# Turning the keys of two batches with one DMA transpose per group of heads

## Chip, cores and metric

One core of one Trainium2 chip runs the program. The metric is the device time of one execution in microseconds (us), the median of three runs. A profiled execution of the same program gives the span (first to last instruction) and the trace from which all rows are taken.

## The reference

Talking-heads attention followed by a gated MLP with spatial mixing, batch B = 4, H = 12 heads, S = 448 positions, D = 64 per head, all inputs and outputs fp32:

```python
scores = scale * np.matmul(q, k.transpose(0, 1, 3, 2))
scores = np.einsum('bhij,hg->bgij', scores, w_pre)
attn = softmax(scores)
attn = np.einsum('bhij,hg->bgij', attn, w_post)
x = np.matmul(attn, v)                       # then (b, s, h*d)
h = gelu(x @ w_in); u, v = split(h)
v_s = w_sg @ layer_norm(v) * g_ln + b_sg
out = x + (u * v_s) @ w_out
```

Matrix products are made of fp16 high and low halves (three products for one fp32 product), or of fp32 operands in the two head mixes where the kernel chooses so.

## The kernel before, in words

**Tiling.** Queries are worked on in chunks: four per batch, of 64, 128, 128 and 128 rows (the first batch a little otherwise, `RUNS`). For each chunk and pair of heads TensorE multiplies qT by kT (`qk_mm`, line 919), ACT and DVE split the scores into halves in the tile s, and SP writes them to a scratch tensor in DRAM (s_d, line 958). They are read back with the heads of ten queries in the partitions (tile g, `load_pair`, line 1019, loads at 1031 and 1037), mixed over heads on TensorE (ps_s), reduced and exponentiated (DVE line 1077, ACT line 1084), mixed again (`postmix`, TensorE tile at), and multiplied by v (ps_av). The MLP of a batch (ps_v, ps_u, ps_x) runs on TensorE between the attention of the next one.

**Keys and queries.** kT holds, for each of three groups of four heads (`hg`, HG = 4), the transposed keys: high and low half (index t), two pairs of heads (index a), 448 columns. For batches 0 and 1 the transposes are made on TensorE (`turns`, line 586). For batches 2 and 3 (`b >= B_DT`) they are made by DMA: `load_k` (line 560) loads four heads of k into a staging buffer st32 (two buffers, ring "st", loads at lines 548 and 550), an engine casts them to the high halves and subtracts for the low halves into the staging buffer st16 (one buffer, ring "sp"; POOL lines 442 and 445 in this program), and `turns_by_dma` (line 567) issues eight DMA transposes on SP: for each half and each pair of heads one of three full blocks of 128 rows (line 580) and one of the last 64 rows (line 582). The load of the next group is planned only when both rings are free, so after the transposes of the group before. The chunks' queries of these batches go through the same single buffer st16 and one DMA transpose of 12 blocks each (`load_q`, line 489). So each batch has three groups of keys, six in all, and four chunks of queries.

**Order.** Nothing is scheduled at run time: a planner (`class Plan`, line 260) simulates the engines with hand-written costs and lists each engine's instructions; each engine then works its list off in order, waiting on semaphores. A step has an engine, a cost, a rank (its due time) and a condition. To each rank a random jitter is added (`JIT` = 0.2, from `random.Random(SEED)`). For a step on SP the cost is the time on the DMA engines, or a pair (that time, number of issues); SP is charged 370 ns for each issue (`SP_ISSUE`), and the planned landing follows from both. SP issues nearly all the kernel's DMAs: writes and reads of scores, loads of k, q, v and weights, transposes, outputs.

**Softmax form.** In the later three batches the second head mix runs with fp16 halves of the probabilities in two of three pairs of query groups and with fp32 operands in the third (`P_F32`).

Of the kernel before, what the change touches and what calls it, by code (L numbers as in the profile page):

```python
# [11 lines left out]
F16 = mybir.dt.float16  # L12
# [31 lines left out]
N_P32 = 3  # L44
N_PRE = 8
C_PRE = 800
SEED = 129
JIT = 0.2
SPIN = 110
SPIN_GAP = 200  # L50
# [57 lines left out]
def talking_heads_gmlp(ctx, tc, q, k, v, w_pre, w_post, w_in, g_ln, w_sg, b_sg, w_out, out):  # L108
    nc = tc.nc
    B, H, S, D = q.shape  # L110
# [3 lines left out]
    P = 128  # L114
# [3 lines left out]
    NC = S // TC  # L118
    JF = S // P
    JL = S - JF * P  # L120
    NA = JF * H + H // 2
    CQ = 120
    NCH = (S + CQ - 1) // CQ
# [13 lines left out]
    HG = 4  # L137
# [6 lines left out]
    ORD = (0, 1, 2, 3)  # L144
# [13 lines left out]
    const = ctx.enter_context(tc.tile_pool(name="const", bufs=1))  # L158
# [55 lines left out]
    mskc_t = vn_hi.rearrange("p c f -> p (c f)")[:, 504:520].bitcast(F32)  # L214


    kT = const.tile([P, H // HG, 2, HG // 2, S], F16, name="kT")
    qT2 = [const.tile([P, 2, H // 2, P], F16, name=f"qT{i}") for i in range(2)]
    v32 = const.tile([P, NA, D], F32, name="v32")
    at32 = const.tile([P, NA, AW], F32, name="at32")  # L220
# [39 lines left out]
    class Plan:  # L260
# [8 lines left out]
        def __init__(self):  # L269
# [7 lines left out]
            self.size = {}  # L277
            self.rnd = random.Random(SEED)

# [6 lines left out]
        def free(self, *names):  # L286
            return self.after([self.res.get(n, 0) for n in names])

        def seen(self, *names):
            return self.after([self.tm.get(n) for n in names])  # L290
# [4 lines left out]
        @staticmethod  # L295
        def after(times):
            return None if None in times else max(times)
# [6 lines left out]
        def give(self, t, *names):  # L304
            for n in names:
                assert self.res[n] is None, n
                self.res[n] = t
# [95 lines left out]
    def ones(n):  # L403

        return {"act": 100 + 0.9 * n, "dve": Shared(70 + 0.52 * n), "pool": 75 + 1.06 * n}
# [28 lines left out]
    free, seen, past, after, take, give, chain = pl.free, pl.seen, pl.past, pl.after, pl.take, pl.give, pl.chain  # L434


    def cast(o, i, scale=1.0, e=None):
        e = e or pl.on
        if e is nc.scalar:
            e.activation(out=o, in_=i, func=AF.Copy, scale=scale)  # L440
        else:
            e.tensor_scalar(out=o, in0=i, scalar1=scale, scalar2=1.0, op0=ALU.mult, op1=ALU.mult)  # L442

    def diff(o, a, b, e=None):
        (e or pl.on).tensor_tensor(out=o, in0=a, in1=b, op=ALU.subtract)  # L445
# [8 lines left out]
    def turn(ps, src, width):  # L454

        for n, x in enumerate(src):
            rows = x.shape[0]
            tr(ps[:, n * width:n * width + rows], x, ident32[:rows, :rows])
# [6 lines left out]

    def turn_k(hg, t, a, ps):
        turn(ps, [t[:, a, cc] for cc in range(JF)] + [t[:JL, a, JF]], P)
        return (ps[:, :S], *(kT[:, hg, k, a, :] for k in range(2)))

    def load_q(i):  # L470
        rank = K_Q12[i - 1] if i < 3 else fin[i - 1] - K_Q
# [49 lines left out]
    def load_kv():  # L521
        todo = [(b * GPB + (0, 3, 6)[hg] + (3 if b else 0), "v", b, hg) for b in range(B) for hg in range(H // HG)]
        for b in range(1, B):
            i = NCH * b - 1
            for hg in range(H // HG):
                todo.append((fin[i] + hg * HG * (fin[i + 1] - fin[i]) // H - K_KV, "k", b, hg))
        todo.sort()
        for rank, kind, b, hg in todo:
            if kind == "v":
                if ("v", b, hg) not in tm:  # L530
                    t = yield "sp", 2000, rank, 0, lambda: seen(("av", b - 1, ORD[-1])) if b else 0
                    fetch_v(b, hg, t)
                continue
            t = yield "sp", 2000, rank, 0, lambda: free(ring("st"), ring("sp"))
            load_k(b, hg, rank + 1, t)

    def fetch_v(b, hg, t):
        hs = slice(hg * HG, (hg + 1) * HG)
        nc.sync.dma_start(out=v32[:, hg * HG * JF:(hg + 1) * HG * JF].rearrange("p (h c) d -> p h c d", c=JF),
                          in_=v[b, hs, :JF * P].rearrange("h (p c) d -> p h c d", c=JF))  # L540
        if hg == H // HG - 1:
            for f in range(2):
                nc.sync.dma_start(out=v32[f * JL:(f + 1) * JL, JF * H:], in_=v[b, f * H // 2:(f + 1) * H // 2, JF * P:].rearrange("h p d -> p h d"))
        tm["v", b, hg] = t

    def fetch_k(b, h0, x):
        hs = slice(h0, h0 + HG)
        nc.sync.dma_start(out=x[:, :, :JF], in_=k[b, hs, :JF * P].rearrange("h (p c) d -> p h c d", c=JF))
        for f in range(2 if b else 1):
            nc.sync.dma_start(out=x[f * JL:(f + 1) * JL, :, JF], in_=k[b, hs, JF * P:].rearrange("h p d -> p h d"))  # L550
# [9 lines left out]
    def load_k(b, hg, rank, t0):  # L560
        h0 = hg * HG
        x, xname = staged("st")
        y, name = staged("sp")
        k32 = y.rearrange("p t a c b d -> p (t a c b d)").bitcast(F32).rearrange("p (a c e) -> p a c e", a=2, c=NC)
        fetch_k(b, h0, x)

        def turns_by_dma(t):
            for part in range(2):
                t = yield None, (ones, twos)[part](HG * NC * D), rank, t
                for a in range(2):  # L570
                    o = y[:, part, :, :, a, :]
                    if part:
                        diff(o, x[:, a::2], y[:, 0, :, :, a, :])
                    else:
                        cast(o, x[:, a::2])
            give(t, xname)
            t = yield "sp", (2500, 5), rank, t, lambda: seen(("qk", NCH * b - 1, h0 + HG - 1))
            for w in range(2):
                for a in range(HG // 2):
                    nc.sync.dma_start_transpose(out=kT[:, hg, w, a, :JF * P].rearrange("p (c j) -> p c j", c=JF),  # L580
                                                in_=y[:, w, a, :JF].rearrange("p c b d -> p (c b d)"))
                    nc.sync.dma_start_transpose(out=kT[:, hg, w, a, JF * P:], in_=y[:JL, w, a, JF].rearrange("p b d -> p (b d)"))  # L582
            give(t, name)
            tm["k", b, hg] = t

        def turns(t):
            t = yield None, ones(HG * NC * D), rank, t
            for a in range(2):
                side(pl.on, k32, x, a)
            give(t, xname)  # L590
            ends = []
            for a in range(2):
                t1 = yield "pe", 4 * C_TR, rank, t, lambda: after([work_free(), seen(("qk", NCH * b - 1, h0 + HG - 1))])
                ps, bank_name = work_bank("ps_k")
                split(rank, t1, turn_k(hg, k32, a, ps), S, bank_name, ends)
            give(t1, name)
            yield None, {"pool": 0}, rank, t1, lambda: max(ends) if len(ends) == 2 else None
            tm["k", b, hg] = max(ends)

        pl.add((turns_by_dma if b >= B_DT else turns)(t0))  # L600
# [6 lines left out]
    def ring(kind):  # L607
        return f"{kind}{stn[kind] % {'st': 2, 'sp': 1}[kind]}"

    def staged(kind):  # L610

        name = ring(kind)
        stn[kind] += 1
        take(name)
        if kind == "st":
            return st32.tile([P, HG, NC, D], F32, tag="st", name="st32"), name
        return st16.tile([P, 2, HG // 2, NC, 2, D], F16, tag="sp", name="st16"), name
# [196 lines left out]
    def work_free():  # L814
        return free(f"wk{works[0] % 2}")
# [47 lines left out]
    def part_mm(s, hg, ps):  # L863
        for n, (tq, tk) in enumerate(((0, 0), (0, 1), (1, 0))):
            for o in range(2):
                for a in range(2):
                    r = slice(a * D, (a + 1) * D)
                    m = QP * (2 * o + a)
                    mm(ps[m:m + QP, :S], lhsT=qT2[0][r, tq, 2 * hg + o, PART[s]:PART[s] + QP],
                                     rhs=kT[r, hg, tk, o, :], start=(n == 0), stop=(n == 2))  # L870

    def part_hi(s, hg, ps, eng=None):
        cast(e0[s][:, hg, 0], ps[:, :S], 1.0 / math.sqrt(D), eng)
# [45 lines left out]
    def qk_mm(i, h, pss):  # L919

        rows = q_rows(i)
        for n, (tq, tk) in enumerate(((0, 0), (0, 1), (1, 0))):
            for o in range(heads(i) // 2):
                w = 64 if quarters(i) else rows
                for c in range(0, rows, w):
                    m = min(w, rows - c)
                    for a, ps in enumerate(pss):
                        r = slice(a * D, (a + 1) * D)
                        mm(ps[o * rows + c:o * rows + c + m, :S], lhsT=qT2[i % 2][r, tq, h // 2 + o, c:c + m],
                                         rhs=kT[r, h // HG, tk, h // 2 % 2 + o, :], start=(n == 0), stop=(n == 2))  # L930

    def qk_place(i, h):
        if (i, h) in early:
# [106 lines left out]
    st = {}  # L1040
# [556 lines left out]
    with tc.manual_schedule():  # L1597
# [13 lines left out]
        for i, w in enumerate((w_pre, w_post)):  # L1611
# [4 lines left out]
                              in_=ident32[:H, :H].unsqueeze(1).unsqueeze(1).to_broadcast([H, 2, NH, H]))  # L1616
# [201 lines left out]
```

## Time and profile before

| | us |
|---|---|
| median of 3 runs | 606.68 |
| lowest, highest of them | 606.08, 610.87 |
| the profiled execution | 607.23 |
| its span | 605.5 |
| TensorE busy in it | 564.6 |
| VectorE (DVE), ScalarE (ACT), GpSimd (POOL) busy | 394.1, 397.1, 284.3 |
| mean granted TensorE clock, share of full | 0.975 |

Times in rows are counted from the start of the span. PE is TensorE, PEld its weight loads, SPq the queue of SyncE, which issues DMAs; a DMA's row on SPq is the time that its issue took. "idle before <-releaser" is how long the engine stood before the instruction and what ended that; of several things waited for, the last by the profile is named, which can be another than the one that mattered.

### The profile page before, as it was taken

To read this page: it belongs to the slowest core of one execution; us is meant where nothing else is said; L and a number is where in the kernel's file an instruction comes from. 1 tells how busy PE (TensorE), PEld (TensorE's weight loads), DVE (VectorE), ACT (ScalarE), POOL (GpSimd) and SP (SyncE) were. 2 spreads that over 40 slices of the span, in tenths; PEclk is the share of its full clock that TensorE was granted. 3 is DMA by queue.
4 is the path that set the end of the run, shared out by engine and by line. 5 is a ranking of instruction groups with operands and counts; after the bars stand their busy time and mean duration, and the time that the engine had idled before them with its cause. 6 is when DMAs were issued, how large, how long until landed. Compare 5 with 4: busy or idle time off the path is not lost.

```text
span 605.5 us, 24600 instructions
## 1 busy us (share of the span) xinstructions
PE 564.6 (93%) x10333; PEld 361.0 (60%) x10333; DVE 394.1 (65%) x991; ACT 397.1 (66%) x952; POOL 284.3 (47%) x421
## 2 busy tenths in 40 slices
PE   8999999999999989299999968789999999999997
PEld 4555666667656546146756635447666656678654
DVE  5866577766887765168878646447678786455560
ACT  5768787886776765256877638446768786765331
POOL 6425255764567572324735735545535474344100
PEclk9999999999999999599999997979999999999999
DMA  8989889995899556689897564689787555430002
GB/s 188 243 249 275 275 259 240 261 273 163 258 265 260 119 158 175 161 215 250 203 282 202 147 208 119 172 195 272 148 241 217 148 180 164 121 87 2 2 2 92
DMA packets 110607, 113.41 MB, mean 187 GB/s; under 512 B 60852, under 2 KB 97724, under 8 KB 110496
## 3 DMA queue, kind: packets, MB, share of 16 engines
q1 hardware_dynamic: 110432, 111.84, 68.3%
q8 instruction: 81, 1.33, 1.0%
q14 instruction: 30, 0.25, 0.1%
q10 hardware_dynamic: 64, 0.00, 0.0%
HBM read 64.20 MB, written 42.10 MB: 176 GB/s over the span
## 4 chain that ended last, share of the span: by engine, by line
PE 47%; SPq 3%; DMA 2%; ACT 1%; DVE 1%; issue 1%; POOL 1%; ACTq 0%; POOLq 0%
PE ps_x L236 9%; PE at L236 8%; PE ps_v L236 7%; PE ps_u L236 7%; PE ps_av L236 6%; PE ps_s L236 5%; PE ps_qk L236 4%; SPq L580 1%; SPq L582 1%; DMA g<-s_d 1%; ACT p L1084 0%; DMA s_d<-s 0%; DMA kT<-st 0%; DVE s L949 0%; ACT at L440 0%
## 5 line engine op out<-in xcount | busy, mean ns | idle before, releaser
L1084 ACT ACTIVATE p<-ps_s,nm 128x448 f32<-128x448 f32 x180 | 113.9, 634 | 33.3 <-DVE nm L1077 30.6
L1077 DVE TENSOR_REDUCE nm<-ps_s 128x1 f32<-128x448 f32 x180 | 105.7, 617 | 41.6 <-PE ps_s L236 41.4
L440 ACT ACTIVATE at<-at 128x420 f32<-128x420 f32 x178 | 97.8, 565 | 32.8 <-PE at L236 31.7
L440 ACT ACTIVATE s<-ps_qk 128x448 f16<-128x448 f32 (+3 forms) x145 | 72.1, 547 | 26.5 <-PE ps_qk L236 21.3
L236 PE MATMUL ps_qk<-kT,qT 64*64 64x448 f16 (+2 forms) x756 | 70.1, 360 | 19.0 <-DMA qT<-st 11.1
L236 PE MATMUL ps_av<-at,v 128*64 128x120 f32 (+3 forms) x1536 | 71.5, 262 | 0.1
L236 PEld LDWEIGHTS ps_av<-at,v 128*64 128x64 f32 (+1 forms) x1536 | 64.8, 136 | 9.3 <-issue 5.8
L236 PEld LDWEIGHTS at<-wp,p 64*64 64x64 f32 (+1 forms) x2580 | 57.1, 139 | 19.3 <-issue 7.4
L442 POOL TENSOR_SCALAR p<-p,rs 128x448 f16<-128x448 f32 (+1 forms) x56 | 39.3, 705 | 54.7 <-DVE rs L1090 33.3
L236 PE MATMUL at<-wp,p 64*64 64x60 f32 (+2 forms) x2580 | 61.7, 224 | 2.8 <-ACT at L440 2.6
L949 DVE SCALAR_TENSOR_TENSOR s<-ps_qk,s 128x448 f16<-128x448 f32 x84 | 48.8, 618 | 22.5 <-ACT s L440 21.2
L236 PE MATMUL ps_u<-xTh,wbuf 128*128 128x256 f16 (+1 forms) x384 | 60.7, 260 | 0.0
L1089 DVE TENSOR_SCALAR rs<-ss 128x1 f32<-128x1 f32 x180 | 26.9, 149 | 49.0 <-ACT p L1084 46.2
L236 PEld LDWEIGHTS <-wbuf 128*128 128x128 f16 x576 | 50.3, 98 | 12.3 <-issue 8.0
L236 PE MATMUL ps_x<-wo,gbuf 128*128 128x384 f16 (+1 forms) x336 | 57.4, 331 | 0.2 <-POOL gbuf L445 0.2
L442 POOL TENSOR_SCALAR wp<-wpc,rs 128x60 f32<-128x60 f32 x63 | 23.2, 368 | 68.8 <-DVE rs L1090 67.5
L236 PEld LDWEIGHTS <-qT 64*64 64x64 f16 (+2 forms) x756 | 23.2, 99 | 54.0 <-issue 24.4
L1113 DVE SCALAR_TENSOR_TENSOR p<-p,rs,p 128x448 f16<-128x448 f32 x58 | 44.7, 773 | 9.3 <-POOL p L442 5.8
L236 PE MATMUL ps_u<-xTl,wbuf 128*128 128x192 f16 (+1 forms) x192 | 49.8, 259 | 0.0
L236 PEld LDWEIGHTS <-p 64*128 64x128 f16 (+1 forms) x2610 | 38.3, 101 | 16.4 <-issue 8.4
L236 PE MATMUL ps_s<-g,wpre 60*64 60x448 f32 x324 | 43.7, 558 | 1.8 <-ACT p L1084 1.8
L236 PEld LDWEIGHTS <-gbuf 128*128 128x128 f16 (+1 forms) x384 | 30.6, 102 | 23.3 <-issue 7.7
(224 smaller groups left out, 1094.5 us busy)
## 6 DMA issues: line engine op xcount, KB each, us to landing
g<-s_d SPq DMA_DIRECT2D x166, 210.0 KB
s_d<-s SPq DMA_DIRECT2D x18, 448.0 KB
s_d<-s SPq DMA_DIRECT2D x24, 280.0 KB
v<-in_v_dram SPq DMA_DIRECT2D x12, 384.0 KB
out_dram<-ot SPq DMA_DIRECT2D x24, 192.0 KB
s_d<-s SPq DMA_DIRECT2D x18, 252.0 KB
s_d<-s SPq DMA_DIRECT2D x18, 224.0 KB
s_d<-s SPq DMA_DIRECT2D x18, 196.0 KB
```

Of the source, the lines that this page charges most:

```text
L236: nc.tensor.matmul(ps, lhsT=lhsT, rhs=rhs, **kw)
L440: e.activation(out=o, in_=i, func=AF.Copy, scale=scale)
L442: e.tensor_scalar(out=o, in0=i, scalar1=scale, scalar2=1.0, op0=ALU.mult, op1=ALU.mult)
L580: nc.sync.dma_start_transpose(out=kT[:, hg, w, a, :JF * P].rearrange("p (c j) -> p c j", c=JF), in_=y[:, w, a, :JF].rearrange("p c b d -> ...
L582: nc.sync.dma_start_transpose(out=kT[:, hg, w, a, JF * P:], in_=y[:JL, w, a, JF].rearrange("p b d -> p (b d)"))
L949: nc.vector.scalar_tensor_tensor(out=e[:, 1, :], in0=ps[:n, :S], scalar=1.0 / math.sqrt(D), in1=e[:, 0, :], op0=ALU.mult, op1=ALU.subtract)
L1077: nc.vector.tensor_reduce(out=nm, in_=st[n]["s2"][:, :S], axis=AX.X, op=ALU.max, negate=True)
L1084: nc.scalar.activation(out=x["p32"], in_=x["s2"][:, :S], func=AF.Exp, bias=x["nm"], accum_out=x["ss"])
L1089: nc.vector.tensor_scalar(out=x["rs"], in0=x["ss"], scalar1=1e-9, scalar2=1.0 / S_P, op0=ALU.add, op1=ALU.mult)
L1113: nc.vector.scalar_tensor_tensor(out=x["pl"], in0=x["p32"], scalar=x["rs"], in1=x["ph"], op0=ALU.mult, op1=ALU.subtract)
```

## The change

kT's columns are padded from 448 to 512, so that a group's 2 halves x 2 pairs x 4 blocks of 128 x 128 lie in one row of equal blocks; the eight transposes of a group become one of 16 blocks, whose last block of each pair is now turned with all its 128 rows (the rows beyond 448 are filled by the load and not read). Readers of kT take the first 448 columns. The planner is told another cost for the key loads (three issues), the last v load of a batch (three issues) and the transposes, and its random seed is another.

```diff
-SEED = 129
+SEED = 23
...
-    kT = const.tile([P, H // HG, 2, HG // 2, S], F16, name="kT")
+    kT = const.tile([P, H // HG, 2, HG // 2, NC * P], F16, name="kT")
...
-        return (ps[:, :S], *(kT[:, hg, k, a, :] for k in range(2)))
+        return (ps[:, :S], *(kT[:, hg, k, a, :S] for k in range(2)))
...
-                    t = yield "sp", 2000, rank, 0, lambda: seen(("av", b - 1, ORD[-1])) if b else 0
+                    t = yield "sp", (2400, 3) if hg == H // HG - 1 else 2000, rank, 0, lambda: seen(("av", b - 1, ORD[-1])) if b else 0
...
-            t = yield "sp", 2000, rank, 0, lambda: free(ring("st"), ring("sp"))
+            t = yield "sp", (2200, 3), rank, 0, lambda: free(ring("st"), ring("sp"))
...
-            t = yield "sp", (2500, 5), rank, t, lambda: seen(("qk", NCH * b - 1, h0 + HG - 1))
-            for w in range(2):
-                for a in range(HG // 2):
-                    nc.sync.dma_start_transpose(out=kT[:, hg, w, a, :JF * P].rearrange("p (c j) -> p c j", c=JF),
-                                                in_=y[:, w, a, :JF].rearrange("p c b d -> p (c b d)"))
-                    nc.sync.dma_start_transpose(out=kT[:, hg, w, a, JF * P:], in_=y[:JL, w, a, JF].rearrange("p b d -> p (b d)"))
+            t = yield "sp", (2800, 5), rank, t, lambda: seen(("qk", NCH * b - 1, h0 + HG - 1))
+            nc.sync.dma_start_transpose(out=kT[:, hg].rearrange("p t a (c j) -> p (t a c) j", c=NC),
+                                        in_=y.rearrange("p t a c b d -> p (t a c b d)"))
...
-                                     rhs=kT[r, hg, tk, o, :], start=(n == 0), stop=(n == 2))
+                                     rhs=kT[r, hg, tk, o, :S], start=(n == 0), stop=(n == 2))
...
-                                         rhs=kT[r, h // HG, tk, h // 2 % 2 + o, :], start=(n == 0), stop=(n == 2))
+                                         rhs=kT[r, h // HG, tk, h // 2 % 2 + o, :S], start=(n == 0), stop=(n == 2))
```

## Rows read from the trace of the kernel before

**Rows 1.** The page: busy time of the engines.
```profile
PE 564.6 (93%) x10333; PEld 361.0 (60%) x10333; DVE 394.1 (65%) x991; ACT 397.1 (66%) x952; POOL 284.3 (47%) x421
```

**Rows 2.** Windows: length, busy PE PEld DVE ACT POOL, then clock, DMA share, GB/s.
```profile
50.00:200.00 150.00, 144.91 (x2561) 95.26 (x2562) 108.77 (x289) 116.38 (x288) 84.51 (x129) 1.00 0.89 250
200.00:300.00 100.00, 85.71 (x1777) 52.50 (x1776) 61.33 (x153) 60.43 (x148) 45.97 (x59) 0.93 0.74 186
...
350.00:400.00 50.00, 35.68 (x662) 21.41 (x655) 24.00 (x59) 23.52 (x55) 22.51 (x28) 0.84 0.61 169
400.00:550.00 150.00, 149.44 (x3132) 97.66 (x3125) 104.11 (x274) 108.58 (x265) 75.11 (x106) 1.00 0.63 173
```

**Rows 3.** TensorE's waits, whole span: waited for: us in total, times, longest.
```profile
PE ps_qk L236 <- DMA qT<-st: 11.1, 1, 11.1
PE ps_s L236 <- ACT p L1084: 9.0, 2, 7.2
PE ps_qk L236 <- DMA kT<-st: 6.2, 3, 2.2
```

**Rows 4.** Chain of waits from 335 to 400 us, by line.
```profile
by line: SPq L580 10.1%; SPq L582 9.4%; DMA g<-s_d 8.8%; PE ps_x L236 8.2%; PE at L236 7.2%; issue 6.6%; PE ps_qk L236 5.5%; PE ps_av L236 5.1%; PE ps_s L236 4.7%; DMA s_d<-s 3.9%; DMA kT<-st 3.6%; SPq L1037 3.0%; SPq L550 2.7%; ACT p L1084
```

**Rows 5.** Timeline of SP's queue: start, duration, line, operation.
```profile
213.82 1.63 SPq L580 DMA_TRANSPOSE kT<-st  x1
...
223.88 1.23 SPq L582 DMA_TRANSPOSE kT<-st  x1
...
227.55 0.42 SPq L548 DMA_DIRECT2D st<-in_k_dram  x1
...
250.27 1.25 SPq L489 DMA_TRANSPOSE qT<-st  x1
...
340.02 1.19 SPq L580 DMA_TRANSPOSE kT<-st  x1
...
353.99 0.42 SPq L548 DMA_DIRECT2D st<-in_k_dram  x1
...
384.59 2.11 SPq L580 DMA_TRANSPOSE kT<-st  x1
```

**Rows 6.** Windows, columns as in rows 2: inside the fourth group's transposes.
```profile
344.00:352.00 8.00, 8.00 (x175) 4.58 (x173) 6.79 (x18) 6.87 (x19) 7.23 (x9) 1.00 0.20 39
```

**Rows 7.** Tile kT: its DMA transposes, ns min/median/max, first and last start.
```profile
L580 SPq DMA_TRANSPOSE kT<-st x24: 1193/1248/2497, 192.6 to 393.2; - x24
L582 SPq DMA_TRANSPOSE kT<-st x24: 1203/1226/2176, 194.1 to 394.5; - x24
```

**Rows 8.** Tile qT: the same for the queries.
```profile
L489 SPq DMA_TRANSPOSE qT<-st x8: 1247/2472/3362, 250.3 to 435.9; - x8
```

**Rows 9.** Timeline of TensorE: idle before and its releaser in brackets.
```profile
253.52 1.33 PE L236 MATMUL ps_qk<-kT,qT 64*64 64x448 f16 x12 [11.12 <-DMA qT<-st]
...
389.52 0.38 PE L236 MATMUL ps_qk<-kT,qT 64*64 64x448 f16 x2
```

**Rows 10.** Timeline of POOL: casts of staged keys and queries.
```profile
213.76 2.27 POOL L445 TENSOR_TENSOR st<-st,st 128x512 f16<-128x512 f32 x2
...
232.98 1.20 POOL L442 TENSOR_SCALAR st<-st 128x512 f16<-128x512 f32 x2 [7.59 <-DMA st<-in_k_dram]
...
247.70 0.82 POOL L442 TENSOR_SCALAR st<-q 64x768 f16<-64x768 f32 x1 [10.66 <-DMA g<-s_d]
...
361.38 1.20 POOL L442 TENSOR_SCALAR st<-st 128x512 f16<-128x512 f32 x2 [9.54 <-DMA g<-s_d]
```

**Rows 11.** SP's own waits from 184 to 250 us.
```profile
SPq L580 <- POOL st L445: 3.2, 3, 1.5
```

**Rows 12.** Windows, columns as in rows 2: after each of the three stalls.
```profile
253.50:260.00 6.50, 6.48 (x102) 3.56 (x103) 2.07 (x6) 3.15 (x8) 3.05 (x3) 0.65 0.73 183
365.40:372.00 6.60, 6.57 (x102) 3.37 (x101) 5.46 (x14) 5.31 (x12) 5.75 (x7) 0.60 0.24 49
396.90:403.00 6.10, 6.10 (x95) 3.45 (x96) 2.52 (x6) 3.06 (x7) 3.06 (x4) 0.63 1.01 228
```

## Prediction

> **What bounds the kernel now.** I read the page first, then five views of the trace, in the order of the row groups. The page has TensorE busy for 564.6 of 605.5 us, the other engines below 70% [rows 1]. So the question is where TensorE stands still, and the windows answer it: from 50 to 200 us it is idle for 5.1 of 150 us, from 400 to 550 for 0.6 of 150; from 200 to 300 it is idle for 14.3 us and from 350 to 400 for 14.3 us, and only there is the granted clock below 1 (0.93 and 0.84) [rows 2]. Those two stretches are where the keys of the third and fourth batch are turned. TensorE's waits name three big pieces: A, 11.1 us on the DMA of qT; B, 7.2 us on ACT's exp; C, 6.2 us in three pieces on the DMA of kT [rows 3].
>
> What lies behind all three is SP, the one queue that issues nearly every DMA. The chain of waits between 335 and 400 us is 10.1% and 9.4% lines 580 and 582, more than any TensorE line [rows 4]. The SP timeline shows how one group of keys passes: eight transposes, first issue at 213.82, last at 223.88 plus 1.23, 11.3 us in which SP issues nothing else; the load of the next keys goes out only at 227.55 [rows 5]. There are six such groups, 48 transposes [rows 7]. Meanwhile the DMA engines do almost nothing: share 0.20 and 39 GB/s from 344 to 352 us, in the middle of one [rows 6]. So the transposes are bound by their issue, not by their bytes.
>
> **The price of a transpose.** By tile, the 24 of line 580 (three blocks of 128 rows) have a median of 1248 ns, the 24 of line 582 (one block of 64 rows) 1226 ns [rows 7]. Six times the data cost 22 ns more: the price hangs on the instruction. A group costs 4 x 1.248 + 4 x 1.226 = 9.9 us at the medians, 11.3 as it ran.
>
> **What replaces it.** One transpose of 16 blocks of 128 rows. The nearest row is line 489, queries, 12 blocks in one instruction (64 or 128 rows): 1.25 us at the least, 2.47 median, 3.36 at the most [rows 8]. Bounds for 16 blocks: 1.25 from below (no smaller than the smaller one), 16/12 x 3.36 = 4.5 from above. I take 2.5, the median of that row. It moves 16 blocks against 3.5 x 4 = 14 of before, as the last block is now turned whole; at share 0.20 over 8 us, 1.6 us of engine time for some 6.4 transposes [rows 6], eight are 2.0 us and the new one 2.3 us. It lands about 2 to 3 us after its issue ends; of qT it is 2.0 (issued at 250.27 for 1.25, TensorE starts at 253.52) [rows 5, 9].
>
> The Trainium skill speaks against the low end: DMA: Bandwidth & Descriptors (Why a DMA increments its semaphore by 16 and not by 1, the table of sequencer time) says that before the newest generation an SBUF transpose took one push per tile, 262,144 cycles for 8,192 of them. By that, 128 tiles of 16 x 128 are 4,096 cycles, an estimate of 3.4 us at the 1.2 GHz that Trainium Kernel Development and Optimization (NeuronCore Architecture) gives SyncE, and the merge saves only the fixed parts. Rows 7 do not agree: 24 tiles against 4 differ by 22 ns, not by 640 cycles. By the rule about 1 us more of each group stays on SP, and the sum below would be some 2 us less gain.
>
> One thing is lost. Before, the first four transposes needed only the high halves and started at 213.82 while POOL was still making the low halves (213.76, 2.27 us) [rows 5, 10]. The single one needs both, so SP stands until 216.0, and what is queued behind it (g loads, writes of s) stands too. SP's waits there are small today, 3.2 us over three groups [rows 11]; the new wait is at most 2.3 us a group. Group 2 then frees SP at 216.0 + 2.5 = 218.5 instead of 225.1: 6.6 us, bounds 4.6 (4.5 us issue) and 7.9 (1.25). A group whose halves are ready saves 7 to 10.
>
> **A, 11.1 us.** qT of the third batch is late because its cast needs the one staging buffer that the third group of keys holds: POOL starts it at 247.70, after 10.66 us of waiting [rows 10]; the row names a g load, but what the cast must have is the buffer. The key cast before it, at 232.98, waited 7.59 us for its own load [rows 10], which SP issued at 227.55 behind group 2. Move that load 6.6 us forward: cast at 226.4, halves done 3.4 us later at 229.8, transpose issued by 232.3 and landed by about 235, query cast and difference 2.6 us (247.70 to the issue at 250.27), qT issued by 240 and landed by 242. TensorE came to wait at 242.4 [rows 9]. At the slow bounds (2.0 us less from group 2, 2.0 us more in each of two transposes) it lands at 248, and A keeps some 5.6 us; but group 1 gives 7 us upstream that I have not counted. A: 11 us gone, bounds 5.5 and 11.1.
>
> **B, 7.2 us.** ACT's exp stands behind its gate cast, that behind POOL's product, and that behind POOL's key cast at 361.38, which waited 9.54 us [rows 10]: its load went out at 353.99, behind eight transposes that began at 340.02 [rows 5]. With 2.5 us in the place of 9.9 it goes out 7.4 us earlier, which covers TensorE's 7.2. All of B goes; at 4.5 us for the transpose 5.4 of it.
>
> **C, 6.2 us.** The three waits are for successive transposes of the sixth group, issued from 384.59 [rows 5]. TensorE's first matmul on it runs at 389.52 [rows 9]. One transpose, issued between 384.6 and 386.9 (the 2.3 us for both halves), lands at 389.6 to 391.9 on its own, which leaves 0.1 to 2.4 us; what groups 4 and 5 save comes on top, also after the 7 us by which TensorE gets there sooner without B. 6.2 us gone, at the bounds 3.8 of it.
>
> **Clock.** After each stall TensorE runs on at the lower level (1.2 instead of 2.4 GHz): 6.48 us busy at 0.65, 6.57 at 0.60, 6.10 at 0.63 [rows 12]. The loss is 6.48 x 0.35 + 6.57 x 0.40 + 6.10 x 0.37 = 2.3 + 2.6 + 2.3 = 7.2 us, gone if the stalls go.
>
> **The rest of the edits.** kT rows padded to 512 change no matmul: same 448 columns. The planner's prices for loads (three issues instead of one) cost no instruction. SEED draws another order for the whole program, all stretches included; this trace has one draw only, so its price is bounded by what orders leave here: 5.1 us idle from 50 to 200 against 0.6 from 400 to 550 [rows 2], that is +-4 us, and I take 0.
>
> **Sum.** 11.1 + 7.2 + 6.2 + 7.2 = 31.7 us at the most. What is late next: the softmax chains and DMA queues that leave 5.1 us in 150 where nothing is turned [rows 2]; some 100 us of such stretch have 3.4 us idle, and with a piece of it long enough to slow the clock I take 4.7. The gain is 27 us. Against the profiled execution (607.2 us, of which 605.5 are the span and the rest lies around it) that is 580.2, against the median of 606.7 it is 579.7: **580 us**.
>
> **Rivals.**
> R1, the gain is half given back. DMA share is 0.89 from 50 to 200 us and 0.74 from 200 to 300 [rows 2]; with the stalls gone the same bytes pass sooner and g loads land late. For: that leaves little room above 0.89. Against: at 0.89 TensorE was still 97% busy. Half of 27 gives 593.
> R2, the merged transpose costs what its parts did: issue by data rather than by instruction, 10 us a group, nothing won, and the wait for both halves added, some 1 us seen of it: 607. Rows 7 and 8 speak against.
> R3, slower: SP, blocked on the low halves, holds its queue. The casts sit in POOL's order behind work that itself waits for a load that SP has not issued. It decides where that wait exceeds the 8 us saved per group; today the largest such POOL wait is 10.7 us [rows 10]. Three groups at 10.7 + 2.3 us with no cover, 39 us, less the 31.7 won: 614. Against: the three SP waits at line 580 total 3.2 us [rows 11].
>
> **How the numbers follow.** Forecast 0.72 (own range 573 to 588: +-4 us of order, -3 us if nothing comes back, +4 if A and C keep their lower bounds), R1 0.18 (588 to 598), R2 0.05, R3 0.05. The range of 8 in 10 runs from 571 (all 31.7 and 4 of order) to 597. About 1%, 6 us, is what a measurement of this kernel can tell from no change. Faster by over 1% (below 600.6): forecast and R1, 0.90. Within 1%: most of R2, 0.05. Slower: R3, 0.05.
>
> **What would show it.** Right: six DMA_TRANSPOSE for kT instead of 48, each 1.3 to 4.5 us long; TensorE idle under 5 us in each of the stretches of A and of B and C together, its wait on qT and kT under 3 us in all; granted clock 0.97 or more there; the kT lines gone from the top of the chain. Wrong: a transposed group that keeps SP for 8 us or more; a wait of 5 us or more on g or on exp in place of A to C; SP waits on the st casts above 15 us in total; or a stretch before 185 us, where no key is turned by DMA, that moves by more than 4 us.

## The result and the profile after

The changed kernel takes 579.8 us (median of 4 runs, 574.6 to 582.2) against 608.0 for the kernel before on the same chip: a ratio of 0.952 with a 95% interval of 0.944 to 0.960. On a second chip (run after_again below) it was 577.2 against 606.8, 0.952 (0.945 to 0.958). The forecast was 580. The profiled execution is the fastest of the four, 574.6 us with a span of 572.9; before it was 607.2 and 605.5, so the two traces lie 32.6 us apart where the medians lie 28.2 apart. Two runs that took over 1.5% more than the fastest of their kernel, 598.4 us in planner_prices and 597.3 in other_draw, are left out of the medians and ratios below.

The windows of the kernel after, columns as in [rows 2]:

```profile
50.00:200.00 150.00, 145.01 (x2647) 96.83 (x2644) 110.00 (x289) 120.15 (x295) 76.82 (x119) 1.00 0.87 246
200.00:300.00 100.00, 98.53 (x1976) 60.43 (x1974) 70.49 (x180) 70.53 (x172) 49.56 (x62) 1.00 0.91 226
300.00:350.00 50.00, 48.63 (x964) 30.22 (x956) 40.08 (x99) 37.76 (x90) 35.17 (x47) 1.00 0.91 232
350.00:400.00 50.00, 49.86 (x1085) 33.95 (x1086) 33.07 (x86) 33.88 (x84) 27.15 (x37) 1.00 0.93 229
```

The stretch before the keys has not moved: TensorE is idle for 5.0 of 150 us, 5.1 before. From 200 to 300 us it is idle for 1.5 us (14.3), from 350 to 400 for 0.1 (14.3), and the granted clock is 1.00 in both (0.93 and 0.84). The DMA engines, 0.74 and 0.61 busy there before, are now at 0.91 and 0.93: the hole that the issue of transposes left is filled.

TensorE's four largest waits from 180 to 400 us, in the columns of [rows 3]:

```profile
PE ps_x L236 <- POOL gbuf L445: 1.3, 2, 1.0
PE ps_av L236 <- ACT s L440: 0.9, 1, 0.9
PE ps_s L236 <- DMA g<-s_d: 0.8, 2, 0.4
PE ps_qk L236 <- DMA kT<-st: 0.5, 1, 0.5
```

Of A (qT), B (exp) and C (kT) 0.5 us on kT is left. The tile kT and the timeline of SP's queue, as in [rows 7] and [rows 5]; line 578 is the merged transpose:

```profile
L578 SPq DMA_TRANSPOSE kT<-st x6: 1716/3124/4518, 210.8 to 358.1; - x6
```

```profile
210.75 3.26 SPq L578 DMA_TRANSPOSE kT<-st  x1
214.10 0.53 SPq L955 DMA_DIRECT2D s_d<-s  x1
214.74 1.18 SPq L1034 DMA_DIRECT2D g<-s_d  x2
215.96 0.46 SPq L548 DMA_DIRECT2D st<-in_k_dram  x1
...
227.90 4.52 SPq L578 DMA_TRANSPOSE kT<-st  x1
...
233.97 0.42 SPq L548 DMA_DIRECT2D st<-in_k_dram  x1
...
243.55 2.89 SPq L578 DMA_TRANSPOSE kT<-st  x1
```

A group keeps SP for 3.3 us on the mean (19.9 us in six rows) where it kept it for 10.9 (65.6 us in 48). From one group's first transpose to the next group's were 21.6 us before (213.82 to 235.44 for groups 2 and 3); they are now 17.2 and 15.7.

How long SP stands in front of a merged transpose has to be read from timelines. The view of waits puts 14.0 us in front of the six, from 184 to 400 us; its longest row is

```profile
SPq L578 <- POOL vs L1504: 7.1, 2, 3.9
```

That view counts up to the release that it infers, and this can lie after the transpose has started: 3.2 of the 7.1 us stand in front of the first group's transpose, whose casts were done before its turn came. The last key casts on POOL for the transposes that start at 210.75, 243.55 and 344.96 us, and SP's queue before the last of these:

```profile
207.27 2.64 POOL L445 TENSOR_TENSOR st<-st,st 128x512 f16<-128x512 f32 x2
...
241.26 2.26 POOL L445 TENSOR_TENSOR st<-st,st 128x512 f16<-128x512 f32 x2
...
342.66 2.27 POOL L445 TENSOR_TENSOR st<-st,st 128x512 f16<-128x512 f32 x2
```

```profile
340.99 1.08 SPq L1034 DMA_DIRECT2D g<-s_d  x2
344.96 1.72 SPq L578 DMA_TRANSPOSE kT<-st  x1
```

The first of these casts ends at 209.91, 0.8 us before its transpose starts, and SP issues loads of g in between (209.85 to 210.66). SP's queue stands empty for a cast only in front of the other two, 1.7 and 2.9 us, and for 1.2 us in front of the fourth group, until TensorE has read the old keys: 5.8 us over six groups.

### The profile page after: what moved, and what is told of

Its sections match the earlier page's. It is cut to its first block, busy times and chain, and to the rows that moved or that the text cites. A ratio compares the mean times of both kernels' runs of the same rounds, so it can differ in the third digit from the quotient of the medians.

```text
span 572.9 us, 24567 instructions
## 1 busy us (share of the span) xinstructions
PE 558.6 (98%) x10335; PEld 360.3 (63%) x10335; DVE 395.0 (69%) x995; ACT 400.5 (70%) x958; POOL 273.7 (48%) x411
## 4 chain that ended last, share of the span: by engine, by line
PE 83%; DMA 6%; ACT 4%; POOL 3%; SPq 2%; issue 1%; DVE 1%; ACTq 0%; POOLq 0%; DVEq 0%
PE at L236 16%; PE ps_x L236 14%; PE ps_s L236 12%; PE ps_av L236 11%; PE ps_v L236 10%; PE ps_u L236 9%; PE ps_qk L236 8%; DMA st<-in_k_dram 2%; DMA kT<-st 1%; ACT p L1081 1%; ACT s L440 1%; ACT at L440 1%; DMA q<-in_q_dram 1%; DMA g<-s_d 1%; DMA s_d<-s 1%
## 5 line engine op out<-in xcount | busy, mean ns | idle before, releaser
L442 POOL TENSOR_SCALAR p<-p,rs 128x448 f16<-128x448 f32 (+1 forms) x53 | 35.5, 671 | 86.9 <-DVE rs L1087 45.0
L236 PE MATMUL ps_qk<-kT,qT 64*64 64x448 f16 (+2 forms) x756 | 68.2, 356 | 1.2 <-DMA kT<-st 0.5
L236 PE MATMUL ps_x<-wo,gbuf 128*128 128x384 f16 (+1 forms) x336 | 55.8, 327 | 1.3 <-POOL gbuf L445 1.3
L236 PE MATMUL ps_u<-xTl,wbuf 128*128 128x192 f16 (+1 forms) x192 | 49.8, 259 | 0.0
L236 PEld LDWEIGHTS <-p 64*128 64x128 f16 (+1 forms) x2610 | 37.0, 99 | 18.9 <-issue 10.1
L1110 DVE SCALAR_TENSOR_TENSOR p<-p,rs,p 128x448 f16<-128x448 f32 x58 | 42.1, 729 | 4.8 <-POOL p L442 4.2
L236 PE MATMUL at<-wpc_hi,p 64*128 64x60 f16 (+1 forms) x1740 | 43.0, 186 | 0.4 <-POOL p L445 0.2
```

Source lines behind the costliest of these rows:

```text
L236: nc.tensor.matmul(ps, lhsT=lhsT, rhs=rhs, **kw)
L1110: nc.vector.scalar_tensor_tensor(out=x["pl"], in0=x["p32"], scalar=x["rs"], in1=x["ph"], op0=ALU.mult, op1=ALU.subtract)
```

## The experiments

Three things were in the change at once: the merge, the planner's prices, and a seed. Theory: SP's time is what the change buys, through the merge alone. Rivals: the new order buys it; or the earlier landing of the keys does, whatever SP does next.

**merge_only**: the kernel before with its seed and its prices, so the same order of instructions on every engine, and the merge, with kT padded as the merge needs it.

```diff
-            for w in range(2):
-                for a in range(HG // 2):
-                    nc.sync.dma_start_transpose(...)
-                    nc.sync.dma_start_transpose(...)
+            nc.sync.dma_start_transpose(out=kT[:, hg].rearrange("p t a (c j) -> p (t a c) j", c=NC),
+                                        in_=y.rearrange("p t a c b d -> p (t a c b d)"))
```

> The kernel before with its own seed and its own planner costs (so the same order of instructions on every engine), and only the eight transposes of a group merged into one. Theory (SP's issue time is what the change buys): 576 to 588 us, most of the 28 us, with TensorE idle under 6 us from 200 us to the end of the fourth batch's key transposes, against 28.6 us before. Rival (the new draw of the order buys it): 600 to 610 us. Rival (half is given back in other waits): 588 to 598 us.

Measured: 576.0 us against 608.8, ratio 0.947 (0.942 to 0.951). Its windows:

```profile
200.00:300.00 100.00, 99.11 (x2108) 61.94 (x2106) 75.40 (x183) 72.46 (x177) 53.59 (x69) 1.00 0.89 223
300.00:350.00 50.00, 47.51 (x933) 30.44 (x931) 38.52 (x94) 35.97 (x87) 33.44 (x42) 1.00 0.81 214
350.00:400.00 50.00, 50.00 (x1120) 32.44 (x1120) 34.54 (x91) 35.54 (x87) 25.03 (x36) 1.00 0.98 229
```

3.4 us of idle time are left of 28.6 from 200 to 400 us. Nothing but the merge and its padding differs, so the two give all of the gain: 32.8 us. Rival one falls. The busy times of merge_only, to be set beside [rows 1]:

```profile
PE 556.8 (97%) x10333; PEld 358.2 (62%) x10333; DVE 397.7 (69%) x991; ACT 396.7 (69%) x952; POOL 284.0 (49%) x421
```

Of 31.6 us less span (605.5 to 573.9), 23.8 are idle time of TensorE and 7.8 its busy time.

**eight_in_new_order**: the changed kernel with the eight transposes put back, into the padded kT.

```diff
-            nc.sync.dma_start_transpose(out=kT[:, hg]..., in_=y...)
+            for w in range(2):
+                for a in range(HG // 2):
+                    nc.sync.dma_start_transpose(...)
+                    nc.sync.dma_start_transpose(...)
```

> The changed kernel with its seed and planner costs, but eight transposes per group again, into the padded kT. Theory: the stalls come back, 598 to 616 us, TensorE idle of 15 us or more between 200 and 400 us, each transpose 1.2 us on SP at the median. Rival (the draw buys it): 575 to 585 us.

Measured: 614.2 us, 1.011 (1.005 to 1.017) of the kernel before. In the order of the changed kernel, too, the merge is worth 34 to 37 us, and as kT is padded here, the padding has no part in it. The stalls are back, now mostly on kT itself; TensorE's waits over the whole span, longest in total first:

```profile
PE ps_qk L236 <- DMA kT<-st: 18.7, 11, 2.4
PE ps_x L236 <- ACT gbuf L440: 4.1, 1, 4.1
PE ps_s L236 <- ACT p L1084: 3.0, 1, 3.0
```

**seed_only**: the kernel before with the new seed.

```diff
-SEED = 129
+SEED = 23
```

> The kernel before with the new seed alone (eight transposes, old planner costs). Theory: within 8 us of the kernel before, 599 to 615 us. Rival (the draw buys it): 575 to 588 us.

Measured: 621.6 us, 1.020 (1.015 to 1.026). The seed buys nothing here, it costs 12.7 us, more than the theory's expectation allowed. An order is worth more than I had taken.

**planner_prices** and **other_draw** measure that with the merge in place: the changed kernel with the old seed, and with a third one.

```diff
-SEED = 23
+SEED = 129
```

> The changed kernel with the old seed, so merge plus the planner's new costs of loads and transposes, which give another order although no jitter is drawn anew. If orders differ by 4 us, as the prediction took: 572 to 584 us. If a new order is worth as much as seed_only showed with eight transposes (13 us): outside of that, up to 590.

```diff
-SEED = 23
+SEED = 1
```

> The changed kernel with a third seed (1). If draws differ as the kernels so far did (576, 577 to 580 and 587 us for three orders with merged transposes): 572 to 592 us.

Measured: 586.6 us, 0.965 (0.959 to 0.971), outside of the 572 to 584 that a swing of 4 us would give, and 590.0 us, 0.971 (0.968 to 0.975). The four orders with merged transposes lie at 576.0 (merge_only), 577.2 and 579.8 (the changed kernel, twice), 586.6 and 590.0: 14 us apart.

**after_again**: the changed kernel once more.

> The changed kernel itself, on the chip of the three others, since its four runs lay 7.6 us apart. 574 to 583 us; against merge_only it is slower by 0 to 6 us, because the draw of the order was no part of the gain.

Measured: 577.2 us (575.5 to 583.1), 0.952 (0.945 to 0.958). Its interval and merge_only's overlap; whether the other edits of the change cost the 1 to 4 us between them, this does not settle.

**hold_sp**: the changed kernel, and behind each merged transpose seven small ones, of 64 rows by 128 of a constant, into a tile that nobody reads. SP is held; a group's own merged transpose, issued before them, is not touched.

```diff
+    junk = const.tile([P, 7, JL], F16, name="junk")
...
+            for n in range(7):
+                nc.sync.dma_start_transpose(out=junk[:, n], in_=ident[:JL])
```

> The changed kernel with seven small transposes more behind each merged one (64 rows by 128 of a constant into a tile that nobody reads, 16 KB each): the SP queue is held for some 7 x 1.23 = 8.6 us more per group, but the merged transpose itself, its bytes and the release of the staging buffer stay as they are. Theory (SP's time): 594 to 610 us, most of the gain gone. Rival (the gain is that keys land and the staging buffer comes free sooner, whatever SP does next): 578 to 588 us.

Measured: 629.7 us, 1.034 (1.027 to 1.042): all of the gain gone and 21 us more. It was expected at 594 to 610. SP's queue shows a part of why:

```profile
215.72 3.10 SPq L579 DMA_TRANSPOSE kT<-st  x1
218.87 10.82 SPq L582 DMA_TRANSPOSE junk<-ident  x7
...
231.72 0.45 SPq L549 DMA_DIRECT2D st<-in_k_dram  x1
```

The seven took 9.6 to 10.8 us in the third batch's groups, not 8.6; with the merged one a group holds SP for 12.9 us on the mean (77.5 in all), where the eight held it for 10.9. The rival of the earlier landing is not settled by this: the next keys' load stands behind the held queue (231.72 us, 215.96 in the changed kernel), so that all later keys land late as well. prefetch_hold_sp_3, below, settles it.

**two_halves**: merge_only with two transposes a group, of 8 blocks each.

```diff
-            nc.sync.dma_start_transpose(out=kT[:, hg]..., in_=y...)
+            for w in range(2):
+                nc.sync.dma_start_transpose(out=kT[:, hg, w].rearrange("p a (c j) -> p (a c) j", c=NC),
+                                            in_=y[:, w].rearrange("p a c b d -> p (a c b d)"))
```

> As merge_only (order of the kernel before), but two transposes per group, high halves and low halves, 8 blocks each. It tells the price of an instruction from the price of its data, and what the wait for both halves costs. Theory (price per instruction, some 1.2 us, plus little for the data): two instructions of 1.2 to 2.5 us each, 574 to 582 us, since two issues keep SP no longer than one loaded one and the first can go before the low halves are made. Rival (price by data): each half as long as half of the merged one, 0.9 to 1.6 us, time as merge_only. Rival (waiting for both halves costs SP much): faster than merge_only by over 3 us.

Measured: 577.2 us, 0.949 (0.943 to 0.954), not to be told from merge_only. Its transposes:

```profile
L579 SPq DMA_TRANSPOSE kT<-st x12: 1239/1436/3432, 195.1 to 364.3; - x12
```

The least for 8 blocks is 1.24 us, as for the small ones of [rows 7], where the merged one's least for 16 is 1.72; a group holds SP for 3.4 us in two instructions and 3.0 in one. By these leasts the price is the instruction's up to 8 blocks, and grows with the data beyond. The first half goes before the low halves are made, and by the timelines SP stands for casts for 3.1 us in all, against 8.1 in merge_only. Nothing is seen to be won by these 5 us, of which the second issue takes 2.5 back; the intervals leave room for a gain of some 3 us.

**hold_sp_3**: merge_only with three small transposes behind each merged one.

```diff
+    junk = const.tile([P, 3, JL], F16, name="junk")
...
+            for n in range(3):
+                nc.sync.dma_start_transpose(out=junk[:, n], in_=ident[:JL])
```

> As merge_only, with three small transposes of a constant behind each merged one: SP is held some 4 us more per group, 24 us in all. hold_sp and the eight-transpose kernels lie on a line of some 0.7 us of time for each us of SP held. Theory A (there is cover up to a point): under 0.3 us per us held, 576 to 584 us. Theory B (every us of SP held in these stretches counts in proportion): 588 to 598 us.

Measured: 596.5 us, 0.981 (0.976 to 0.987), 20.4 us over merge_only for 26.0 us that SP was held more (43.8 against 17.8): 0.79 us for each. No cover shows: theory B. SP's queue and POOL's timeline show one way by which it goes:

```profile
217.22 2.98 SPq L579 DMA_TRANSPOSE kT<-st  x1
220.26 4.89 SPq L582 DMA_TRANSPOSE junk<-ident  x3
226.76 0.42 SPq L549 DMA_DIRECT2D st<-in_k_dram  x1
```

```profile
233.94 1.20 POOL L443 TENSOR_SCALAR st<-st 128x512 f16<-128x512 f32 x2 [7.32 <-DMA st<-in_k_dram]
```

The next group's load stands behind the held queue and POOL waits 7.3 us for it. At the end of the chain TensorE waits for the queries, as in A:

```profile
PE ps_qk L237 <- DMA qT<-st: 13.8, 3, 7.5
```

**hold_after_load** asks whether that chain carries all of it: merge_only and the same three, issued right behind the group's key load and not between a transpose and the next load.

```diff
+    junk = const.tile([P, 3, JL], F16, name="junk")
...
         fetch_k(b, h0, x)
+        if b >= B_DT:
+            for n in range(3):
+                nc.sync.dma_start_transpose(out=junk[:, n], in_=ident[:JL])
```

> As merge_only, with the same three small transposes per group as hold_sp_3, but issued right behind the group's key load instead of behind its transpose: SP is held as long, in the 8 us in which the chain of a group is with the load's landing and POOL's cast, and not between a transpose and the next group's load. Theory (the cost runs through the chain load, cast, transpose, next load): at most 8 us over merge_only, 577 to 584 us. Rival (SP's time counts wherever it is spent, by the g loads and s writes queued behind it): 590 to 600 us, as hold_sp_3 (596.5). In between: both.

Measured: 588.2 us, 0.969 (0.964 to 0.974). 12.2 us over merge_only for 32.0 us held (49.8 in all): 0.38 for each. Its largest wait of TensorE:

```profile
PE ps_s L237 <- DMA g<-s_d: 5.2, 3, 3.5
```

Both, then: about half the price is left. Where SP is held matters, and 5.2 us of what is left show as waits on loads of g (0.2 in merge_only).

**prefetch** and **prefetch_hold_sp_3** ask the same in another way: merge_only, in which the next keys are loaded as soon as a buffer st32 is free, with and without the three small transposes behind the merged one.

```diff
-            t = yield "sp", 2000, rank, 0, lambda: free(ring("st"), ring("sp"))
+            t = yield "sp", 2000, rank, 0, lambda: free(ring("st"))
...
-        y, name = staged("sp")
...
-                t = yield None, (ones, twos)[part](HG * NC * D), rank, t
+                t = yield None, (ones, twos)[part](HG * NC * D), rank, t, lambda: 0 if part else free(ring("sp"))
+                if not part:
+                    y, name = staged("sp")
...
```

> As merge_only, but the next group's keys are loaded as soon as one of the two staging buffers st32 is free, and the one buffer st16 is asked for only at the cast; before, the load waited in the plan for both. The planner makes another order of it. Theory (load, cast, transpose of one group stand in one chain with the next group's, so whatever is put on SP between them counts): 568 to 590 us, new order included, with POOL's waits on the key loads from 184 us on gone (they are 1.7, 3.3 and 4.8 us in merge_only). Its own time tells little; the pair with the next kernel tells.

> The kernel prefetch with the three small transposes behind each merged one, in the same order of instructions as prefetch. Theory (the chain over the next group's load carries the cost of a held SP): this is at most 8 us slower than prefetch, where the same edit cost merge_only 20 us. Rival (a held SP costs through all that is queued there, loads of g and writes of s above all): 16 to 24 us slower than prefetch.

Measured: 591.7 us, 0.974 (0.969 to 0.979), just above what was expected, and 605.7 us, 0.999 (0.997 to 1.002): 14.0 us for 34.1 us held (48.6 against 14.6), 0.41 for each, between the two expectations and the same answer as hold_after_load. The pair also settles the rival of the earlier landing: with the hold, the third batch's merged transposes start at 201.0, 212.2 and 223.9 us, without it at 202.5, 213.2 and 222.8. The keys are turned as early, and yet the batch's next queries are turned at 236.7, 246.0 and 259.1 us in place of 231.1, 239.6 and 252.1: what stands behind the hold pays.

POOL's waits on the key loads are gone in prefetch, but its order costs more than it gives: a wait of TensorE that is 1.3 us in merge_only,

```profile
PE at L236 <- POOL p L445: 5.7, 1, 5.7
```

and it is 15.7 us slower than merge_only. Loading the keys sooner is no gain in this order.

Held time of SP (all key and small transposes of the profiled execution, added up from its timeline; in two_halves without the waits between the halves) against the median time. The kernels ran on several chips, on which the kernel before took 606.8 to 608.8 us; the slopes are against the first kernel of the same order. Taken from the ratios instead, hold_after_load has 0.42, and the others move by 0.03 at most:

| order of | kernel | SP held, us | time, us | us per us held |
|---|---|---|---|---|
| before | merge_only | 17.8 | 576.0 | |
| before | two_halves | 20.3 | 577.2 | inside the interval |
| before | hold_after_load | 49.8 | 588.2 | 0.38 |
| before | hold_sp_3 | 43.8 | 596.5 | 0.79 |
| before | the kernel before | 65.6 | 608.8 | 0.69 |
| changed | the changed kernel | 19.9 | 579.8 | |
| changed | eight_in_new_order | 64.7 | 614.2 | 0.77 |
| changed | hold_sp | 77.5 | 629.7 | 0.87 |
| prefetch | prefetch | 14.6 | 591.7 | |
| prefetch | prefetch_hold_sp_3 | 48.6 | 605.7 | 0.41 |

## Why the prediction was right, and where it was not

**What bounds it: right.** SP's issue is the thing. Merging in the same order gives 32.8 us, taking the merge out of the changed kernel gives 34 back, and holding SP with transposes that do nothing takes the whole gain.

**The price of a transpose: right in kind, low in size.** The prediction had 2.5 us for the merged one, between 1.25 and 4.5. It took 3.12 at the median, 1.72 to 4.52, and 19.9 us for six where 15 were reckoned; in after_again one took 5.05, beyond the upper bound. The price is the instruction's only for few blocks. The leasts are 1.24 us for 8 blocks (two_halves), 1.4 for 12 of 128 rows (the 1.25 of [rows 8], taken as the lower bound, is a chunk of 64 rows) and 1.72 for 16. What comes on top goes with the load on the DMA engines, which the prediction did not name. The longest and the shortest of the six, in the columns of [rows 2]:

```profile
227.90:232.42 4.52, 4.52 (x117) 3.32 (x114) 2.35 (x6) 2.72 (x8) 0.05 (x1) 1.00 1.20 191
344.96:346.68 1.72, 1.72 (x22) 0.48 (x20) 1.00 (x5) 0.66 (x3) 1.72 (x2) 1.00 0.31 65
```

The DMA share is 1.20 in the one and 0.31 in the other; in the four between it is 0.82 to 1.11. The rule of the Trainium skill that was weighed there (DMA: Bandwidth & Descriptors, Why a DMA increments its semaphore by 16 and not by 1, the table of sequencer time) would have 32 cycles for each of the 64 tiles between 8 and 16 blocks, an estimate of 1.7 us at 1.2 GHz. Measured are 0.48 us between the leasts, which a fixed price per tile does not allow; the medians (1.44 and 3.12), with the load in them, are 1.7 us apart.

**The wait for both halves: right to be small, by a row that does not show it.** The 3.2 us of [rows 11] are counted as the 14.0 above are, up to releases after the transposes had started; by the timeline SP's queue stood empty for 0.5 us in front of the third batch's transposes (before 213.82), so the waits before were smaller than reckoned. The bound of 2.3 us a group was passed in single groups (2.9 in the changed kernel, 4.1 in merge_only), but in all SP stands for casts for 4.6 us, and 8.1 in merge_only: below the 15 us that would have shown the prediction wrong.

**A, B and C: right.** All three are gone and did not turn up elsewhere; 0.5 us on kT is left. In merge_only, the same order, qT of the third batch is issued at 236.0 us; the prediction had "by 240". With C, B and A the slower clock went too: 1.00 in all windows from 50 us on. The sizes hold in merge_only: TensorE's idle time fell by 23.8 us, where A, B and C made 24.5, and its busy time by 7.8, where the clock was reckoned at 7.2.

**The sum: right by two sizes that were off, which is luck.** "What is late next" was put at 4.7 us. In merge_only it is nothing that the interval shows: 32.8 us measured, 31.7 reckoned at the most. In its place stands what the prediction called the rest of the edits, "+-4 us, and I take 0": the orders with merged transposes lie 14 us apart, those with eight 13 (608.8, 614.2, 621.6). A swing of some 7 us either way is what that term should have had, and the range with it. The idle times of two stretches of one trace, from which I took the 4, say nothing of how another order fares. That the changed kernel has an order 1 to 4 us behind the old one is what brought the number to 580; with other_draw's seed it would have been 590, in the range of R1 and without R1's cause.

**R1** (half given back) did not come: the DMA engines stand at 0.91 and TensorE at 98%. **R2** (10 us a group, by data) is excluded by the merged rows of 1.7 to 4.5 us. **R3** (slower, a held queue) did not come: no wait for a cast came near the 8 us saved per group. What a queue held for longer than before costs is seen in hold_sp, where another cause holds it.

**Left open.** How the price of a held SP divides. Two kernels in which the next keys' load does not stand behind the hold pay 0.38 and 0.41 us per us, those in which it does 0.69 to 0.87. So the chain load, cast, transpose, next load carries about half, as far as these two tell; which of the other transfers carry the rest (loads of g and of q, writes of s) was not tried one by one. The small transposes also put 16 KB each on the DMA engines; by the prediction's 2.0 us of engine time for eight, an estimate of 4.5 us for 18. What of the price is due to that, no run tells apart.

## What to carry to other kernels

A DMA has a price on the queue that issues it, and when that queue issues nearly all transfers, instructions can cost more than bytes: look for stretches in which the DMA engines are at 0.2 and the queue has no gap, and try putting several small transfers of one kind into one instruction first. To see what such a queue is worth, add instructions to it that do nothing: the slope tells, and moving them tells which successor pays. Where a planner orders the program by hand-set costs, compare one edit in one fixed order; a new draw of the order can be worth as much as a third or half of a good change. And set a view of waits beside the starts in the timeline: a wait that ends after the start is none.

## What the runs showed that was not expected

A held SP costs although its queue has gaps: 0.79 us per us in hold_sp_3, with 4.3 us held more in a group, while in merge_only gaps of over 0.2 us in SP's timeline add up to 62 of the 216 us from 184 to 400. A queue with idle time in it is not a queue with slack. Smaller holds were not measured: the 2.5 us in all that two_halves holds more are lost in the noise.

Executions also differ before any added instruction can act: hold_sp_3's profiled execution issues its first load of keys for a DMA transpose at 187.81 us, merge_only's at 184.10, in the same order; in the first 50 us the granted clock was 0.93 in the one and 1.00 in the other. The window of hold_sp_3, columns as in [rows 2]:

```profile
0.00:50.00 50.00, 47.38 (x528) 24.98 (x529) 31.62 (x73) 30.35 (x68) 20.71 (x51) 0.93 0.85 213
```

The same window of merge_only:

```profile
0.00:50.00 50.00, 46.53 (x581) 25.72 (x581) 33.94 (x79) 33.75 (x76) 22.10 (x54) 1.00 0.89 231
```

What makes TensorE start at the lower level in one execution and not in another was not tried.
